# The tail of an attention and SwiGLU backward pass: how pairs of token tiles are scaled, summed and copied

## The chip, the cores and the metric

The kernel runs on one core of one Trainium2 chip. A core has a matrix engine (TensorE, PE in the profile, with PEld for its weight loads), VectorE (DVE), ScalarE (ACT), GpSimd (POOL), a queue engine that issues transfers (SyncE, SP), and 16 DMA engines. The engines run side by side, each its own instructions in order, and wait for each other by semaphores. The on-chip memories are SBUF (128 partitions) and PSUM, into which TensorE writes its results. The metric is the time of one execution on the device in microseconds (us); runs are summed up by their median.

## The reference

A transformer block with both branches on the same normalised input, and the gradients of its inputs. S = 2048 tokens, D = 448, 16 heads of 28, F = 1792, everything bfloat16.

```python
xn = layernorm(x)                      # no weights, eps 1e-5
qkv = xn @ wqkv                        # 448 x 1344
p = softmax(q @ k.T * 28 ** -0.5);  o = p @ v
out = x + o @ wo + (silu(xn @ w_gate) * (xn @ w_up)) @ w_down
grads = vjp(out)(grad_out)             # for x, wqkv, wo, w_gate, w_up, w_down
```

The outputs are out and six gradients. What matters here: with dqkv the gradient of q, k and v, the gradient of wqkv is xn^T dqkv, and the gradient of xn is dqkv wqkv^T plus the part from the FFN. With g that sum for one token, the gradient of x is rstd * (g - mean(g) - xn * mean(g * xn)) + grad_out.

## The kernel before

The forward pass (0 to about 618 us) computes attention for four groups of four heads and, as filler work between, the FFN. Then comes the turn, and the backward pass of attention: 512 steps, each a group g, a pair of heads hp, a chunk kc of 512 keys, a chunk qc of 512 queries and a tile qi of 128 queries. `row(k)` computes scores and dP of a step on TensorE, `ew(k)` the exponential on ScalarE and ds = dP * e on VectorE (L842), `kv(k)` accumulates dk and dv, and `dq_unit(b)` dq for a block of four steps. dq needs ds transposed. For the tiles 0 to 2 of a block a DMA does this (`dst_dma`, issued by SP, L823 and L827), for tile 3 TensorE, in `tr_unit` (L878, copied by ScalarE at L879). Between the steps TensorE gets filler units (y, FFN part of dx, and `dc_unit`, L1149), in an order that is written out by hand.

At the turn, the pieces of the last units of the forward pass (`last[-5:]`: 16 pieces of dO wo^T, L482; three of small VectorE work; 16 of the gradient of wo, L518) are taken one by one, counted in n, and the steps 0 to 3 of the backward pass are started between them, when n % 8 == 1.

After the last step comes the tail (from about 1429 us), for 16 tiles of 128 tokens in eight pairs:

- `dx_a(t0)` sums the gradient of xn in PSUM (tile "tok", six buffers). dqT (L1273) and dkv (L1277) are the last group's. The rest of the sum already lies in SBUF as dxg (fp32). For an even tile VectorE adds dxg and sums the row (L1291); for an odd one TensorE adds dxg by a matmul with the identity in fp32 (L1280), and ScalarE sums the row (gs, L1288). In both cases VectorE forms the product with xn and its row sum (pr, L1294); its input is dxg in SBUF for an even tile and tok in PSUM for an odd one.
- `dx_b(t)`, one pair later, scales the two row sums by rstd and -1/D (two [128, 1] instructions of VectorE, L1301), forms t1 on ScalarE (L1304) and t2 on VectorE (L1307), adds them on GpSimd (L1309) and stores the tile (SP, L1310). t1 and t2 take turns in five buffers called e_sb.
- The list `rest` holds the last group's weight gradient of wqkv: two `dsp_unit` and two `dsq_unit` (8 transposes each and a copy by VectorE, L978 and L959) and four `dwq_unit` (16 matmuls of 384 columns, L988, and four casts by VectorE, L994 to L997). Two units are taken in each iteration over t, one behind each place of a `dx_b`, from the first iteration on (which has no `dx_b` yet), so all eight are through after four iterations: the four of transposes at t = 0 and 2, two `dwq_unit`s at t = 4 and two at t = 6.

Of the kernel before, what the change touches and what calls it, by code (L numbers as in the profile page):

```python
# [9 lines left out]
ALU = mybir.AluOpType  # L10
# [20 lines left out]
CH = 256  # L31
NCH = S // CH
QH = 256
LO = 44
HOT = 150

# [66 lines left out]
def kernel(  # L103
# [222 lines left out]
    def run(u):  # L326
        for _ in u:
            pass
# [501 lines left out]
    def ew(k):  # L830
        if k < NB:
            est[k] = kq.tile([P, 2, 512], BF16, name="e_sb", bufs=5)
            for j in range(2):
                ACTE.activation(out=est[k][:, j], in_=sps.pop((k, j))[:], func=ACT.Exp, scale=SCALE)  # L834
        if 1 <= k <= NB:
            g, hp, kc, qc, qi = steps[k - 1]
            b = (k - 1) // 4
            if qi % 2 == 0:
                dss[k - 1] = dss[k] = kq.tile([P, 2, 2, 512], BF16, name="ds_sb", bufs=5)
            ds = dss[k - 1]  # L840
            for j in range(2):
                DVE.tensor_tensor(out=ds[:, qi % 2, j], in0=dps.pop((k - 1, j))[:], in1=est[k - 1][:, j], op=ALU.mult)  # L842
            if qi == 1 or qi == 2:
                if bk is None:
                    pend.append(lambda: dst_dma(b, ds, qi))
                else:
                    dst_dma(b, ds, qi)
# [10 lines left out]
    for u in last[-5:]:  # L858
        for _ in u():
            n += 1  # L860
            if n % 8 == 1 and k < 4:
                row(k)
                ew(k)
                k += 1
# [8 lines left out]

    def tr_unit(b):
        ds = dss.pop(4 * b + 3)
        ps = ps_b.tile([P, 8, P], BF16, name="db", bufs=3)
        for c in range(8):
            PE.transpose(ps[:, c, :], ds[:, 1, c // 4, (c % 4) * P:(c % 4 + 1) * P], ident_bf[:])  # L878
        ACTE.copy(out=dsT[b][:, 3].rearrange("p j kt s -> p (j kt) s"), in_=ps[:])  # L879

    def kv(k):
        g, hp, kc, qc, qi = steps[k]
# [83 lines left out]
    def dsp_unit(g, kind, t8, tag="genb"):  # L966
        if g not in dsp:
            need(lambda: g == 0 or (g - 1, 3) in s_done)
        if g not in dsp:
            dsp[g] = bk.tile([P, NT, 3, P], BF16, name="dsp", bufs=1)  # L970
        src = dkv[g, kind - 1]
        ps = (ps_b if tag == "rest" else ps_g).tile([P, 8, P], BF16, name=tag, bufs=2 if tag == "rest" else 1)
        for j in range(8):
            t = 8 * t8 + j
            PE.transpose(ps[:, j, :], src[:, t * P:(t + 1) * P], ident_bf[:])
            if j < 7:
                yield 60
        DVE.tensor_copy(out=dsp[g][:, 8 * t8:8 * t8 + 8, kind, :], in_=ps[:])  # L978
        s_done.add((g, kind, t8))
        yield 60  # L980

# [2 lines left out]
    def dwq_unit(g, c, tag="genb"):  # L984
# [6 lines left out]
                yield 162  # L991
        o = bk.tile([P, 3, 4, DH], BF16, name="dwq_o")
        p4 = ps[:].rearrange("p (k h r) -> p k h r", k=3, r=HP)
        DVE.tensor_copy(out=o[:dn, 0], in_=p4[:dn, 0, :, :DH])  # L994
        DVE.tensor_copy(out=o[:dn, 1:3, 0:2, :], in_=p4[:dn, 1, :, :DH].rearrange("p (k h) r -> p k h r", k=2))
        DVE.tensor_copy(out=o[:dn, 2, 2:4, :], in_=p4[:dn, 2, 0:2, :DH])
        DVE.tensor_copy(out=o[:dn, 1, 2:4, :], in_=p4[:dn, 2, 2:4, :DH])  # L997
        store(wq_out[d0:d0 + dn, :, g * 4 * DH:(g + 1) * 4 * DH],
              o[:dn].rearrange("p k h r -> p k (h r)"))
        s_done.add((g, c))  # L1000
# [262 lines left out]
    g = G - 1  # L1263
    both = [(dkv[g, 0], wqT[:, 3 * g + 1]), (dkv[g, 1], wqT[:, 3 * g + 2])]

    def dx_a(t0):
        for t in (t0, t0 + 1):
            pst = ps_b.tile([P, 512], FP32, name="tok", bufs=6)
            psd[t] = pst[:, :D]
        for hp in range(2):  # L1270
            for t in (t0, t0 + 1):
                r = 64 * (t % 2)
                PE.matmul(psd[t], lhsT=dqT[g][r:r + 64, hp, t // 2 * P:(t // 2 + 1) * P], rhs=dxs["wqd"][r:r + 64, hp],  # L1273
                          start=(hp == 0), stop=False, tile_position=(r, 0), skip_group_check=True)
        for t in (t0, t0 + 1):
            for i, (l, r) in enumerate(both):
                PE.matmul(psd[t], lhsT=l[:, t * P:(t + 1) * P], rhs=r, start=False, stop=(i == 1 and t % 2 == 0),  # L1277
                          skip_group_check=True)
            if t % 2:
                PE.matmul(psd[t], lhsT=ident_f[:], rhs=dxs["g"][:, t, :], start=False, stop=True, skip_group_check=True)  # L1280
        for t in (t0, t0 + 1):
            ps = psd[t]
            sa = tw.tile([P, 1], FP32, name="sa", bufs=6)
            sb = tw.tile([P, 1], FP32, name="sb", bufs=6)
            sms[t] = (sa, sb)
            if t % 2:
                gs = tw.tile([P, D], BF16, name="gs")
                ACTE.activation(out=gs[:], in_=ps, func=ACT.Identity, accum_out=sa[:])  # L1288
            else:
                psd[t] = dxs["g"][:, t, :]  # L1290
                DVE.scalar_tensor_tensor(out=psd[t], in0=ps, scalar=1.0, in1=psd[t],  # L1291
                                         op0=ALU.mult, op1=ALU.add, accum_out=sa[:])
            pr = tw.tile([P, D], BF16, name="pr")
            DVE.scalar_tensor_tensor(out=pr[:], in0=psd[t], scalar=1.0, in1=xn_sp[:, t, :],  # L1294
                                     op0=ALU.mult, op1=ALU.mult, accum_out=sb[:])

    def dx_b(t):
        ps = psd.pop(t)
        sa, sb = sms.pop(t)
        for x in (sa, sb):  # L1300
            DVE.tensor_scalar(out=x[:], in0=x[:], scalar1=rstd[:, t:t + 1], scalar2=-1.0 / D,  # L1301
                              op0=ALU.mult, op1=ALU.mult)
        t1 = kq.tile([P, 512], FP32, name="e_sb", bufs=5)[:, :D]
        ACTE.activation(out=t1, in_=ps, func=ACT.Identity, scale=rstd[:, t:t + 1], bias=sa[:])  # L1304
        t2 = kq.tile([P, 512], FP32, name="e_sb", bufs=5)[:, :D]
        dy = dy2[t // 4][:, t % 4, :] if t < 8 else dy4[:, t - 8, :]
        DVE.scalar_tensor_tensor(out=t2, in0=xn_sp[:, t, :], scalar=sb[:], in1=dy, op0=ALU.mult, op1=ALU.add)  # L1307
        dx = tw.tile([P, D], BF16, name="dx")
        POOL.tensor_tensor(out=dx[:], in0=t1, in1=t2, op=ALU.add)  # L1309
        SP.dma_start(out=out1_d[:, t, :], in_=dx[:])  # L1310

    rest = [dsp_unit(g, 2, t8, "rest") for t8 in range(2)]
    rest += [dsq_unit(g, hp, "rest") for hp in range(2)]
    rest += [dwq_unit(g, c, "rest") for c in range(4)]
    for t in range(0, NT + 2, 2):
        if t < NT:
            dx_a(t)
        for u in (t - 2, t - 1):
            if u >= 0:
                dx_b(u)  # L1320
            if rest:
                run(rest.pop(0))
    for u in rest:
        for _ in u:
            pass
    tlst.close()
    dxgst.close()
    bwd.close()
# [30 lines left out]
```

## Time and profile before

| what | us |
|---|---|
| median of 12 runs | 1484.97 |
| lowest and highest of them | 1481.98, 1496.54 |
| the profiled execution | 1483.37 |
| its span, first to last instruction | 1481.6 |
| busy: PE, ACT, DVE, POOL | 1350.0, 1262.8, 1159.3, 361.4 |
| tail, from the first L1273 to the end of the span | 1429.65 to 1481.6 |
| start of the last store (L1310) | about 1478.6 |

A profile is one execution. Its rows give the start and the duration of instructions in microseconds from the span's start. Durations of neighbouring rows of one engine overlap a little, so what an instruction occupies is better read from the starts. "x4" is a count; in brackets stands how long the engine was idle before, and who ended it. L12 is line 12 of the kernel before. In the page's shares, an engine's share of the whole span says little about the tail: there PE is at 0 from about 1461 on. PEclk is the clock that TensorE was granted, as a share of full speed.

### The profile page before, as it was taken

Reading aid. Unit: us, or ns where it says so; the run is one execution under the profiler, and the core shown is the slowest. Engines: PE = TensorE matmul, PEld = TensorE weight load, DVE = VectorE, ACT = ScalarE, POOL = GpSimd, SP = SyncE. Lnnn points to the kernel's source line nnn. Section 1 sums busy time; section 2 is a strip of 40 time slices with the busy share of each in tenths; the row PEclk is TensorE's granted clock in tenths of the full one; section 3 lists DMA queues with packets and bytes.
Section 4 is the critical chain, followed back from the end, with each engine's and each line's share of the span. In section 5 each row is a group of like instructions: output and inputs, shape, how many; then the busy total and the mean of one; then the engine's idle time right before and its main releaser. Section 6 shows DMA issues by size and latency. Waiting matters only on the chain. (4 is left out here: it accounts for less than half of the span.)

```text
span 1481.6 us, 34337 instructions
## 1 busy us (share of the span) xinstructions
PE 1350.0 (91%) x12672; PEld 542.2 (37%) x12672; DVE 1159.3 (78%) x2030; ACT 1262.8 (85%) x2180; POOL 361.4 (24%) x487
## 2 busy tenths in 40 slices
PE   5899999889999999888999889999999998999994
PEld 2333333333333333323333334433343343443341
DVE  6677666556666766587888879888889999999987
ACT  5798989888999998688888879899889998889953
POOL 6474423463434444101001001001001010000113
PEclk9999999999999999988999989999999999999997
DMA  5797856696788676699999999999999999999961
GB/s 149 171 209 184 206 117 157 158 209 161 154 179 189 138 173 142 169 204 195 203 198 201 206 206 189 196 208 215 215 186 200 203 211 214 199 194 211 185 122 50
DMA packets 698591, 269.55 MB, mean 182 GB/s; under 512 B 618080, under 2 KB 674104, under 8 KB 698424
## 3 DMA queue, kind: packets, MB, share of 16 engines
q1 hardware_dynamic: 693448, 261.24, 86.5%
q0 software_dynamic: 3568, 5.83, 1.7%
q8 instruction: 99, 1.62, 0.5%
q14 instruction: 68, 0.56, 0.1%
q10 hardware_dynamic: 1408, 0.30, 0.1%
HBM read 63.99 MB, written 58.85 MB: 83 GB/s over the span
## 5 line engine op out<-in xcount | busy, mean ns | idle before, releaser
L842 DVE TENSOR_TENSOR ds_sb<-db,e_sb 128x512 bf16<-128x512 f32 x1024 | 648.3, 684 | 70.9 <-PE db L815 29.2
L834 ACT ACTIVATE e_sb<-sb 128x512 bf16<-128x512 f32 x1024 | 554.1, 611 | 62.2 <-PE db L815 45.3
L608 ACT ACTIVATE eT<-s_w 128x1024 bf16<-128x1024 f32 x256 | 263.4, 1029 | 49.1 <-PE s_ps L605 46.3
L610 ACT ACTIVATE eT<-s_ps 128x512 bf16<-128x512 f32 x512 | 280.2, 612 | 0.0
L815 PE MATMUL db<-kd,qd 32*128 32x512 bf16 x1024 | 242.3, 389 | 17.1 <-DVE ds_sb L842 16.2
L807 PE MATMUL sb<-kd,qd 32*128 32x512 bf16 x1024 | 214.1, 392 | 5.5 <-ACT e_sb L834 3.3
L938 POOL TENSOR_TENSOR dq_acc<-dq_acc,dq_st 128x256 f32<-128x256 f32 x64 | 46.5, 727 | 586.2 <-ACT dq_st L936 586.2
L896 PE MATMUL acc<-ds_sb,qd 128*32 128x512 bf16 x1024 | 165.2, 400 | 0.0
L892 PE MATMUL acc<-e_sb,qd 128*32 128x512 bf16 x1024 | 163.2, 400 | 1.6 <-DVE dw_o L523 1.6
L879 ACT COPY dsT<-db 128x1024 bf16<-128x1024 bf16 x128 | 130.1, 1017 | 28.6 <-PE db L878 27.7
L377 POOL TENSOR_TENSOR nn<-nn,ag 128x512 f32<-128x512 f32 x56 | 71.3, 1272 | 247.2 <-DVE ag L375 237.6
L605 PE MATMUL s_ps<-QQ,KK 32*128 32x512 bf16 x512 | 125.9, 385 | 4.1
L1105 PE MATMUL genb<-wguT,dau_c 128*128 128x448 bf16 x448 | 117.5, 355 | 6.3 <-ACT dq_st L936 3.3
L605 PE MATMUL s_w<-QQ,KK 32*128 32x512 bf16 x512 | 100.3, 387 | 11.6 <-ACT eT L608 10.0
L807 PEld LDWEIGHTS <-qd 32*128 32x128 bf16 x1024 | 48.3, 91 | 149.7 <-issue 140.8
L416 PE MATMUL gen<-xn_t,f_sp 128*128 128x448 bf16 x448 | 98.5, 354 | 1.2 <-DVE hda L405 1.1
L923 PE MATMUL genb<-dsT,kd 128*32 128x256 bf16 x2048 | 82.8, 284 | 7.3 <-DVE y L1057 3.8
L416 PEld LDWEIGHTS <-f_sp 128*128 128x128 bf16 x672 | 58.7, 98 | 81.5 <-issue 29.6
L878 PE MATMUL db<-ident_bf,ds_sb 128*128 128x128 bf16 x1024 | 80.5, 223 | 1.8 <-DVE ds_sb L842 1.8
L878 PEld LDWEIGHTS <-ds_sb 128*128 128x128 bf16 x1024 | 69.1, 100 | 27.4 <-issue 8.8
L378 POOL TENSOR_TENSOR nn<-nn,tt 128x512 f32<-128x512 f32 x56 | 71.8, 1283 | 4.4
L923 PEld LDWEIGHTS <-kd 128*32 128x32 bf16 x2048 | 56.9, 100 | 43.7 <-issue 15.5
(157 smaller groups left out, 1882.3 us busy)
## 6 DMA issues: line engine op xcount, KB each, us to landing
F_d<-hda SPq DMA_DIRECT2D x56, 384.0 KB
dau_c<-F_d SPq DMA_DIRECT2D x56, 256.0 KB
h_c<-F_d SPq DMA_DIRECT2D x24, 256.0 KB
qd<-QD_d SPq DMA_DIRECT2D x24, 256.0 KB
dc<-dqkvT_d SPq DMA_DIRECT2D x12, 384.0 KB
dsT<-ds_sb SPq DMA_TRANSPOSE x256
wT_d<-wT_f SPq DMA_DIRECT2D x14, 256.0 KB
KD_d<-qk_sp SPq DMA_DIRECT2D x7, 512.0 KB
```

The costliest lines, as they stand in the source:

```text
L416: PE.matmul(ps[:, :D], lhsT=fsp[fc][:, t // 4, w, t % 4, :], rhs=rhs[:, t, :], start=(t == 0), stop=(t == NT - 1))
L605: PE.matmul(sp4[hh], lhsT=KK[g][r:r + HP, kt * P:(kt + 1) * P], rhs=QQ[g][r:r + HP, qsl], start=True, stop=True, tile_position=(r, 0))
L608: ACTE.activation(out=e2[0][:], in_=wide[:], func=ACT.Exp, scale=SCALE)
L610: ACTE.activation(out=e2[1][:, j], in_=sp4[2 + j], func=ACT.Exp, scale=SCALE)
L807: PE.matmul(s_ps[:], lhsT=qside[g, qc][r:r + HP, 0, qi * P:(qi + 1) * P], rhs=kside[g, kc][r:r + HP, 0, :], start=True, stop=True, tile_po ...
L815: PE.matmul(d_ps[:], lhsT=qside[g, qc][r:r + HP, 1, qi * P:(qi + 1) * P], rhs=kside[g, kc][r:r + HP, 1, :], start=True, stop=True, tile_po ...
L834: ACTE.activation(out=est[k][:, j], in_=sps.pop((k, j))[:], func=ACT.Exp, scale=SCALE)
L842: DVE.tensor_tensor(out=ds[:, qi % 2, j], in0=dps.pop((k - 1, j))[:], in1=est[k - 1][:, j], op=ALU.mult)
L878: PE.transpose(ps[:, c, :], ds[:, 1, c // 4, (c % 4) * P:(c % 4 + 1) * P], ident_bf[:])
L892: PE.matmul(a[r:r + HP, :], lhsT=sp4[:, 1, r:r + HP], rhs=e[:, j, :], start=first, stop=last, tile_position=(0, r), skip_group_check=True)
L896: PE.matmul(a[r:r + HP, :], lhsT=sp4[:, 0, r:r + HP], rhs=ds[:, qi % 2, j, :], start=first, stop=last, tile_position=(0, r), skip_group_ch ...
L923: PE.matmul(ps[r:r + HP, :256], lhsT=ks[:, kt, h:h + HP], rhs=t[:, par::2, j, kt, :], start=(kt == 0), stop=(kt == 3), tile_position=(0, r ...
```

## The change

Six edits:

1. At the turn, steps 0 to 3 are started at n = 8, 17, 25 and 32 instead of 1, 9, 17 and 25.
2. In the last block of the backward pass tile 2 of ds is transposed by TensorE too; its copy is made by VectorE. SP issues one transposition less.
3. Tiles 0, 2, 4 and 6 to 12 (EVEN) add dxg on VectorE; 1, 3, 5, 13, 14 and 15 by the matmul with the identity. So of the pairs (6, 7), (8, 9) and (10, 11) both tiles are summed on VectorE, and of (14, 15) none.
4. The four row sums of a pair lie in one [128, 2, 2] tile and are scaled by one instruction, against nrs = -rstd / D, made once by GpSimd. t2 gets buffers of its own (ds_sb), dx four. The last tile's addition is on VectorE. In `dx_a` the dqT matmuls come last.
5. The units of `rest` stand behind both `dx_b` of an iteration: two each at t = 0 and 2, then one `dwq_unit` each at t = 4, 6, 8 and 10 (before: two each at t = 0, 2, 4 and 6).
6. The four casts of the last `dwq_unit`s, and the second copy of `dsp_unit`, are made by ScalarE.

```diff
-            if qi == 1 or qi == 2:
+            if qi == 1 or qi == 2 and b < NB // 4 - 1:
...
-            if n % 8 == 1 and k < 4:
+            if n in (8, 17, 25, 32):
...
+        for qi in (3,) if b < NB // 4 - 1 else (2, 3):
+            ps = ps_b.tile([P, 8, P], BF16, name="db", bufs=3)
+            for c in range(8):
+                PE.transpose(ps[:, c, :], ds[:, qi % 2, c // 4, (c % 4) * P:(c % 4 + 1) * P], ident_bf[:])
+            o = dsT[b][:, qi].rearrange("p j kt s -> p (j kt) s")
+            if qi == 2:
+                DVE.tensor_copy(out=o, in_=ps[:])
+            else:
+                ACTE.copy(out=o, in_=ps[:])
...
+        (ACTE.copy if tag == "rest" and t8 else DVE.tensor_copy)(out=dsp[g][:, 8 * t8:8 * t8 + 8, kind, :], in_=ps[:])
...
+        cp = ACTE.copy if tag == "rest" else DVE.tensor_copy
+        cp(out=o[:dn, 0], in_=p4[:dn, 0, :, :DH])
...
+    nrs = tw.tile([P, NT], FP32, name="nrs", bufs=1)
+    POOL.tensor_scalar(out=nrs[:], in0=rstd[:], scalar1=-1.0 / D, scalar2=None, op0=ALU.mult)
...
     def dx_b(t):
         ps = psd.pop(t)
-        sa, sb = sms.pop(t)
-        for x in (sa, sb):
-            DVE.tensor_scalar(out=x[:], in0=x[:], scalar1=rstd[:, t:t + 1], scalar2=-1.0 / D,
-                              op0=ALU.mult, op1=ALU.mult)
+        sm = sms[t - t % 2]
+        if t % 2 == 0:
+            DVE.tensor_tensor(out=sm[:], in0=sm[:], in1=nrs[:, t:t + 2].unsqueeze(2).to_broadcast([P, 2, 2]), op=ALU.mult)
+        sa, sb = sm[:, t % 2, 0:1], sm[:, t % 2, 1:2]
...
-        t2 = kq.tile([P, 512], FP32, name="e_sb", bufs=5)[:, :D]
+        t2 = kq.tile([P, 2, 512], FP32, name="ds_sb", bufs=5)[:, 0, :D]
...
-        dx = tw.tile([P, D], BF16, name="dx")
-        POOL.tensor_tensor(out=dx[:], in0=t1, in1=t2, op=ALU.add)
+        dx = tw.tile([P, D], BF16, name="dx", bufs=4)
+        (DVE if t == NT - 1 else POOL).tensor_tensor(out=dx[:], in0=t1, in1=t2, op=ALU.add)
...
+    at = {0: 2, 2: 2, 4: 1, 6: 1, 8: 1, 10: 1}
     for t in range(0, NT + 2, 2):
         if t < NT:
             dx_a(t)
         for u in (t - 2, t - 1):
             if u >= 0:
                 dx_b(u)
-            if rest:
-                run(rest.pop(0))
+        for _ in range(at.get(t, 0)):
+            run(rest.pop(0))
```

## The prediction, made before the changed kernel was run

> **What bounds the kernel now.** I read the table of busy time by stretches first, to find where the engines stop being full; then the chain that ended last; then the tail's order of time, row by row.
>
> ```profile
> 1410.00:1420.00 10.00, 10.00 (x114) 4.14 (x117) 9.83 (x18) 9.47 (x18) 1.00 (x2) 1.00 0.91 130
> 1420.00:1430.00 10.00, 8.08 (x110) 3.70 (x102) 5.55 (x12) 5.22 (x8) 0.00 (x0) 0.83 0.88 160
> 1444.00:1448.00 4.00, 4.00 (x24) 1.93 (x23) 2.29 (x10) 0.64 (x2) 1.13 (x1) 1.00 0.37 100
> 1464.00:1468.00 4.00, 0.00 (x0) 0.00 (x0) 3.73 (x12) 1.53 (x3) 1.79 (x2) 0.58 0.17 57
> 1472.00:1476.00 4.00, 0.00 (x0) 0.00 (x0) 3.68 (x10) 1.71 (x4) 2.55 (x3) 0.50 0.09 30
> ```
>
> The columns are the stretch, its length, and the busy time of PE, PEld, DVE, ACT and POOL, then PE's clock, the DMA share and GB/s. Up to 1420 three engines are full, and the change leaves the instructions of that loop as they are. At 1444 to 1448 PE is full and DVE half idle; from 1464 PE has nothing left and DVE alone is full. So the tail has a stage set by PE (about 1444 to 1458) and one set by DVE (1458 to 1477). The chain that ended last is DVE work to the end but for the last POOL addition:
>
> ```profile
> 1475.93 1.40 DVE e_sb L1307
> 1477.33 0.03 POOLq L1309
> 1477.36 0.07 issue
> 1477.43 1.15 POOLq L1354
> ```
>
> One pair of token tiles in the stage of DVE, from the tail in order of time (start, duration, engine, line, instruction):
>
> ```profile
> 1463.59 0.61 DVE L1291 SCALAR_TENSOR_TENSOR dxg<-tok,dxg 128x448 f32<-128x448 f32 x1
> 1463.80 1.13 POOL L1309 TENSOR_TENSOR dx<-e_sb 128x448 bf16<-128x448 f32 x1 [0.61 <-ACT gs L1288]
> ...
> 1464.24 1.17 DVE L1294 SCALAR_TENSOR_TENSOR pr<-dxg,xn_t 128x448 bf16<-128x448 f32 x1
> ...
> 1465.34 0.61 DVE L1294 SCALAR_TENSOR_TENSOR pr<-tok,xn_t 128x448 bf16<-128x448 f32 x1
> ...
> 1466.32 0.68 DVE L1307 SCALAR_TENSOR_TENSOR e_sb<-xn_t,sb,dsT 128x448 f32<-128x448 bf16 x1
> ...
> 1467.14 1.13 POOL L1309 TENSOR_TENSOR dx<-e_sb 128x448 bf16<-128x448 f32 x1 [2.21 <-DVE sa L1301]
> ...
> 1467.37 1.38 DVE L1307 SCALAR_TENSOR_TENSOR e_sb<-xn_t,sb,dsT 128x448 f32<-128x448 bf16 x1
> ```
>
> The same L1307 takes 0.68, or 1.38 when an addition of POOL is running; L1294 takes 0.61 with its input from PSUM and 1.17 when both inputs are in SBUF and POOL is running. 1467.37 to 1468.75 ends 0.48 after POOL's 1467.14 + 1.13 = 1468.27, most of a free instruction: DVE waited for POOL. From dxg to dxg a pair takes 1468.67 - 1463.59 = 5.08.
>
> **The change, part by part.** Starts of neighbouring DVE rows give what each occupies: dxg 0.65 with its accumulator row, a product 0.55, a last scaling (L1307) 0.61, a small scaling (L1301) 0.12, plus 0.1 until the next instruction sees it.
>
> *Turn from forward to backward (the condition on n).* Rows 0 to 3 go behind the 8th, 17th, 25th and 32nd piece of work, not the 1st, 9th, 17th and 25th. The first matmul that needs the accumulators waits for the copy of dw_o, which DVE does at 627.42. From 620.44 on DVE has no gap before that copy, and the work before it is the same, only in another order; its one idle stretch (0.55, before 620.44) becomes about 0.4, the time until PE has done all 16 pieces and the product can start. Gain 0.15. The small operations of the last forward block move ahead of two ds products, so SP gets its transposition 1.2 earlier; it is hidden, nobody waits for SP before 640. I take 0.2, with -2 to +2, for what a shifted start may do to transfers.
>
> *Last ds by TensorE.* SP loses one transposition (1.94 of issue), PE gains 8 transposes (0.53 to 0.9 by the rows of L878), DVE one copy of 128x1024 (0.68, row L978). PE does wait for that transfer: L923 waits 1.24 and starts at 1429.10. But look at what is late next: PE starts the transposes at 1426.33, 16 of them last until 1427.75; the dq matmuls of the block before run to 1428.4 and DVE's dqT after them to 1428.92 (0.42), and only then is the one PSUM bank free; ScalarE's copy of the last quarter ends at 1429.06. So the last dq starts at 1429.1 as before: 0, between -0.5 (PE at full clock) and +0.5.
>
> *Tail, PE.* Two of the eight additions of dxg by an fp32 matmul go (0.76 each in starts), the dqT matmuls come last in a tile, and after the first pairs there is one dwq unit (2.7 by L988: 16 matmuls) in an iteration instead of two. Before, an iteration had 2 x 2.7 + 2.0 = 7.4 (the starts at 1444.82 and 1452.23 are 7.41 apart); now it has 2.7 + 1.25 = 3.95 and is below DVE's.
>
> *Tail, ScalarE.* 16 casts of dwq_o and one 128x1024 copy come from DVE, two gs go. A copy of 128x256 takes 0.38 to 0.43 (L936) and 448 columns 0.54 (L1288), so 112 columns about 0.26 and 56 about 0.22: some 0.75 to 1.0 a unit. ScalarE was busy 1.5 of 4. What is queued behind a unit's casts is the next pair's t1, or gs of tile 13; the matmuls they wait for end 3 us before their turn. Hidden; without that cover each unit would cost up to 1.
>
> *Tail, DVE.* 32 small scalings go for 8 of 128x4 (0.24 each with the wait for it); 16 casts and one copy go (4 x 0.62 + 0.62); 2 dxg of 0.65 come, and the last addition (0.6). A pair whose two tiles are both summed on DVE is then 2 x (0.65 + 0.555) + 0.24 + 2 x 0.61 = 3.87, without POOL.
>
> *POOL against DVE.* [...] The row: DVE's two-input instruction waits until POOL's addition ends, and the 16 additions last 1.13 each:
>
> ```profile
> L1309 POOL TENSOR_TENSOR dx<-e_sb x16: 1127/1130/1137, 1437.3 to 1477.5; 128x448 bf16<-128x448 f32 x16
> L378 POOL TENSOR_TENSOR nn<-nn,tt x56: 1264/1271/1592, 56.4 to 594.5; 128x512 f32<-128x512 f32 x56
> ```
>
> By the first of these alone POOL is never held. [...] The 1592 of L378 beside its median of 1271 is a hint that POOL can be held; I take both directions. Then such a pair runs: addition 1 starts at the end of the second t2; dxg 0.65; the product waits 1.13 - 0.65 = 0.48; when it ends, addition 2 starts; dxg, again 0.48. 3.87 + 2 x 0.48 = 4.83. With DVE held and POOL never held, additions start 0.5 earlier, and the tail below ends some 3.2 earlier.
>
> Now the stretches, each to the end of a t2 (before: rows of L1307; after: the instructions of each engine laid end to end in their new order with the durations above).
>
> - 1429.65 to t2 of tile 3 (1444.07): 14.4. After: PE reaches the end of its second pair 5.25 in (two pairs of 2.0, two transposing units of 0.53); then DVE does two products, scaling, two t2, two copies, dxg, the held product (0.44), a product, scaling, two t2: 8.1. Sum 13.4.
> - to tile 7 (1458.59): 14.5, set by PE. After: two DVE pairs, 9.7.
> - to tile 9 (1463.67): 5.1. After: 4.8.
> - to tile 11: 5.1. After, with tile 13 summed by TensorE: 0.65 + 0.48 + 0.555, then addition 2 holds the scaling for 1.13, + 0.24 + 1.22 = 4.3.
> - to tile 13 (1473.83): 5.1. After: the scaling waits for two additions, 2 x 1.13 + 0.08, + 0.24 + 1.22 = 3.8.
> - to the last addition (1478.58): 4.75. After: addition, t2, addition alternate: 1.26 + 1.13 + 2 x 0.61 + 1.13 + 0.62 = 5.4. The last addition on DVE saves 0.5 here.
>
> Sum 49.0 before, 41.4 after: 7.6 less. The store behind it keeps its 3.0 (1478.6 to 1481.6). With the turn, 7.8 off the span of 1481.6, giving 1473.8. That execution took 1483.37; the median of the runs is 1484.97, 1.6 above. Subtracting from the median: 1477.2.
>
> **Rivals.** *POOL is never held*, as its 16 equal rows suggest: 11.0 off, 1474. *The gain is cut by half*: the two sums on DVE bring two held products to each pair, four pairs in the middle; if DVE must also let POOL's second addition go first (another 1.13 for each of three pairs), 7.8 - 3.4 = 4.4 remains: 1480.5. [...] For it speaks that DVE idles behind POOL already; against it, that DVE's instruction asks first, 0.48 ahead. *Slower*: the clock of PE after the turn. Its rows:
>
> ```profile
> 640.00:650.00 10.00, 8.90 (x101) 3.35 (x101) 7.54 (x14) 8.90 (x17) 0.00 (x0) 0.83 1.07 195
> 650.00:660.00 10.00, 7.93 (x80) 3.00 (x78) 8.81 (x15) 9.18 (x18) 0.00 (x0) 0.96 1.06 198
> 660.00:664.00 4.00, 4.00 (x41) 1.19 (x42) 2.28 (x4) 2.75 (x6) 0.00 (x0) 0.50 1.22 210
> ```
>
> At half clock PE is full and DVE does 2.28 in 4 us instead of about 3.5, a loss of 0.35 us per us. [...] It decides from 8 / 0.35 = 23 more us at half clock, and with 35 the time is 1489. Against it: PE's idle gap at the turn (1.55) doesn't grow.
>
> **How the numbers follow.** As worked out, 0.60 (1475 to 1479.5); POOL not held, 0.12 (1472.5 to 1475); cut by half, 0.21 (1479.5 to 1483); slower, 0.07. The range leaves out the last and the ends of the second and third: 1473 to 1482.5. A measurement of this kernel tells about 0.3%, 4.5 us, from no change; faster therefore means below 1480.5. Faster: 0.60 + 0.12 + 0.08 = 0.80; same: 0.13; slower: 0.07.
>
> **What would show it.** Right: tail pairs of 4.8 between equal t2 rows in the middle; PE's last matmul near 1459 and no more full stretch of PE after 1445; POOL's first addition of a pair starting at the end of the second t2; the last dq matmuls still near 1429.1; the last DVE addition near 1471. Wrong: additions that start while a t2 runs and keep 1.13 (POOL not held, faster); products of 1.7 or scalings waiting over 1.2 (cut by half); DVE rows waiting for gs or PE for casts on ScalarE; a backward loop that reaches 1420 later than before (clock).

## The result, and the profile after

The changed kernel takes 1469.94 us (median of 11 runs, 1467.69 to 1474.87) against 1484.52 us (median of 47 runs of the kernel before, 1474.93 to 1496.54): a ratio of 0.9903, 95% interval 0.9886 to 0.992, that is 11.9 to 16.9 us less. The forecast was 7.8 us less, with a range of 1473.0 to 1482.5. The direction was right, the size was not.

The profiled execution took 1469.94 us, its span 1468.1 (before 1481.6). Where the 13.5 us between the two spans lie, in marks that both traces have:

| from, to | before | after | less |
|---|---|---|---|
| start of the span, last ds product (L842, L843 after) | 1423.85 | 1421.91 | 1.94 |
| last ds product, last dq matmuls (L923, L929 after) | 5.25 | 3.70 | 1.55 |
| last dq matmuls, first matmul of the tail | 0.55 | 0.55 | 0 |
| first matmul of the tail, end of the span | 51.95 | 41.94 | 10.01 |

"The tail" below is always the last of these rows. The first row scatters by several us from execution to execution, as is shown further down; the last hardly does.

The busy time by stretches of the changed kernel (columns as before: stretch, length, PE, PEld, DVE, ACT, POOL, clock, DMA share, GB/s), at places that answer to those shown before:

```profile
1410.00:1420.00 10.00, 10.00 (x121) 4.00 (x120) 9.83 (x18) 9.53 (x18) 0.99 (x2) 1.00 1.01 160
1420.00:1430.00 10.00, 8.72 (x118) 5.24 (x117) 6.16 (x14) 4.70 (x8) 0.00 (x0) 1.00 0.77 188
...
1446.00:1450.00 4.00, 4.00 (x27) 2.20 (x25) 3.82 (x10) 1.91 (x6) 2.40 (x3) 1.00 0.28 79
...
1454.00:1458.00 4.00, 1.41 (x7) 0.32 (x6) 3.22 (x8) 2.56 (x8) 2.95 (x4) 0.92 0.24 68
1458.00:1462.00 4.00, 0.00 (x0) 0.00 (x0) 3.78 (x9) 1.92 (x5) 2.95 (x4) 0.50 0.18 57
```

Where DVE was half idle beside a full PE (busy 2.29 of 4 us), it is now at 3.82 of 4. PE ends at 1455.4, 29.25 after the tail's first matmul (before 31.69), and DVE carries the rest. The chain that ended last is DVE's last addition:

```profile
1463.66 0.09 issue
1463.75 0.05 DVEq L1319
1463.80 0.04 issue
1463.84 1.28 DVE dx L1319
```

One pair whose two tiles are both summed on DVE, in order of time (start, duration, engine, line, instruction; "x2" is two instructions in one row):

```profile
1447.43 1.28 DVE L1317 SCALAR_TENSOR_TENSOR ds_sb<-xn_t,sm,dsT 128x448 f32<-128x448 bf16 x2
1448.35 2.83 POOL L1319 TENSOR_TENSOR dx<-e_sb,ds_sb 128x448 bf16<-128x448 f32 x2 [1.60 <-ACT e_sb L1314]
1448.63 0.62 DVE L1301 SCALAR_TENSOR_TENSOR dxg<-tok,dxg 128x448 f32<-128x448 f32 x1
...
1449.29 0.90 DVE L1304 SCALAR_TENSOR_TENSOR pr<-dxg,xn_t 128x448 bf16<-128x448 f32 x1
...
1450.12 0.61 DVE L1301 SCALAR_TENSOR_TENSOR dxg<-tok,dxg 128x448 f32<-128x448 f32 x1
...
1450.78 0.89 DVE L1304 SCALAR_TENSOR_TENSOR pr<-dxg,xn_t 128x448 bf16<-128x448 f32 x1
...
1451.85 1.28 DVE L1317 SCALAR_TENSOR_TENSOR ds_sb<-xn_t,sm,dsT 128x448 f32<-128x448 bf16 x2
```

From t2 to t2 a pair takes 1451.85 - 1447.43 = 4.42, where 4.83 was forecast and 5.08 stood before. The two t2 of this pair are not held: 1.28 together. POOL's first addition starts 0.92 behind the first t2, into the second one, and is itself held: the two additions take 2.83 instead of 2 x 1.13. The products wait for POOL, but take 0.90 and 0.89 instead of 0.62: a wait of 0.28, not the 0.48 of the forecast. The additions and these products over the whole kernel (shortest, median, longest in ns):

```profile
L1319 POOL TENSOR_TENSOR dx<-e_sb,ds_sb x15: 1123/1357/1515, 1434.2 to 1463.3; 128x448 bf16<-128x448 f32 x15
...
L1304 DVE SCALAR_TENSOR_TENSOR pr<-dxg,xn_t x10: 624/890/1118, 1429.0 to 1453.7; 128x448 bf16<-128x448 f32 x10
```

Before, the additions were 1127/1130/1137. So POOL is held now, for the first time in this tail.

### The profile page after: what moved, and what is told of

Same layout as the page of the kernel before. It is cut to its first block, busy times and chain, and to the rows that moved or that the text cites. A ratio compares the mean times of both kernels' runs of the same rounds, so it can differ in the third digit from the quotient of the medians.

```text
span 1468.1 us, 34327 instructions
## 1 busy us (share of the span) xinstructions
PE 1349.8 (92%) x12676; PEld 541.7 (37%) x12676; DVE 1152.6 (79%) x1995; ACT 1264.1 (86%) x2193; POOL 362.3 (25%) x487
## 5 line engine op out<-in xcount | busy, mean ns | idle before, releaser
L843 DVE TENSOR_TENSOR ds_sb<-db,e_sb 128x512 bf16<-128x512 f32 x1024 | 648.4, 684 | 70.0 <-PE db L816 33.1
L929 PE MATMUL genb<-dsT,kd 128*32 128x256 bf16 x2048 | 82.6, 283 | 5.4 <-DVE y L1064 2.9
L929 PEld LDWEIGHTS <-kd 128*32 128x32 bf16 x2048 | 56.9, 100 | 41.6 <-issue 15.3
```

Of the source, the lines that this page charges most:

```text
L929: PE.matmul(ps[r:r + HP, :256], lhsT=ks[:, kt, h:h + HP], rhs=t[:, par::2, j, kt, :], start=(kt == 0), stop=(kt == 3), tile_position=(0, r ...
```

## The experiments

The theory that the runs were to test: the gain lies in the tail and comes of the pair on DVE (one scaling, copies on ScalarE, the units of weight gradients apart), with POOL and DVE each made to wait for the other. ("Port" in what was expected of the runs is the author's word for whatever the two wait for; the runs show who waits and for how long, not at what.) The rivals: the gain comes of the turn or of the last ds; or the tail's gain has one cause alone. The tail of three executions with the same tail code and TensorE at full clock (the changed kernel, the run without the new turn, the run with needless transposes below) is 41.94, 41.99 and 41.94. One execution is therefore enough for a difference of half a us in the tail, though not for the time of the whole kernel.

**The parts alone.** Four kernels, each against the same 37 runs of the kernel before (median 1484.86).

The tail edits (3 to 6) alone: the changed kernel with the turn, the issue of the last ds and `tr_unit` as before:

```diff
-            if n in (8, 17, 25, 32):
+            if n % 8 == 1 and k < 4:
...
-            if qi == 1 or qi == 2 and b < NB // 4 - 1:
+            if qi == 1 or qi == 2:
```

> The tail's edits alone, without the turn's and without the last ds on TensorE. Theory A (the tail carries nearly all): the two traces give 49.0 us before and 39.5 after from the last dq to the last addition, so 9.5 to 10.5 off the median. Theory B (the tail gave what was forecast, 7.6, and the rest lies in the loop or the last ds): 7 to 8.

Measured: 1475.05 us (median of 6), ratio 0.9914 (0.9893 to 0.9936). The tail is 42.86, and the last dq starts 5.25 behind the last ds product.

The new turn alone, put into the kernel before:

```diff
-            if n % 8 == 1 and k < 4:
+            if n in (8, 17, 25, 32):
```

> The kernel before with only the turn's condition changed. Theory A: 0, within 1. Theory B (the new start of the backward loop is worth what the trace of after is ahead at its end, 2 to 3 us): 2 to 3.5 off.

Measured: 1482.89 us (16 runs), ratio 0.9986 (0.9969 to 1.0002), which includes no change.

The last ds by TensorE alone, put into the kernel before, with the changed `tr_unit`:

```diff
-            if qi == 1 or qi == 2:
+            if qi == 1 or qi == 2 and b < NB // 4 - 1:
```

> The kernel before with only the last block's third tile transposed by TensorE. My forecast of this step was 0, because PE would only start the last dq at the same time. By the trace of after it starts 1.5 earlier in relation to the last ds product. Theory A (the gain is real: without the transfer PE goes on at full clock and without the 1.24 wait): 1 to 2 off, and the last dq starts 5.2 behind the last ds product. Theory B (TensorE's clock fell at that place in the trace of before by chance): 0 to 0.5, and the start depends on the clock.

Measured: 1484.08 us (22 runs), ratio 0.9978 (0.9958 to 0.9998): at the edge of what can be told; the two medians differ by only 0.8 us. Its last dq came 5.05 behind the last ds product, with a stretch of half clock between the two.

All but the turn:

```diff
-            if n in (8, 17, 25, 32):
+            if n % 8 == 1 and k < 4:
```

> The changed kernel with the turn as before. Theory A: the time of the changed kernel, 1469 to 1471. Theory B: 2 to 3.5 more, 1472 to 1473.5.

Measured: 1470.16 us (4 runs), ratio 0.9887 (0.9871 to 0.9902), tail 41.99. It can't be told from the changed kernel. The tail carries the gain; the turn adds nothing that can be told, the last ds little.

**Each edit of the tail put back.** Four kernels, one execution each: the changed kernel with one edit undone.

The weight-gradient units two at a time again:

```diff
-    at = {0: 2, 2: 2, 4: 1, 6: 1, 8: 1, 10: 1}
+    at = {0: 2, 2: 2, 4: 2, 6: 2}
```

> The changed kernel with the units of the weight gradient as before: two each in the iterations t = 0, 2, 4, 6. Length of the tail = from the first matmul of the first pair to the end of the span: 51.95 before (1429.65 to 1481.6), 41.94 after (1426.16 to 1468.1). Theory A (one unit per pair takes PE out of the bound): 3.5 to 4.5 longer, PE full between 1440 and 1450. Theory B (DVE's savings carry the gain, the place of the units matters little): under 1 longer.

Measured: tail 46.45, 4.5 more. The groups by shape say why: sums of DVE wait 8.4 us for TensorE instead of 2.9. First the changed kernel,

```profile
L1301 DVE SCALAR_TENSOR_TENSOR dxg<-tok,dxg 128x448 f32<-128x448 f32 x10 | 6.2, 618 | 2.9 <-PE tok L1291 2.9
```

then the run (the numbers behind the bars: busy us and mean ns of one; idle us before them and who ended it):

```profile
L1301 DVE SCALAR_TENSOR_TENSOR dxg<-tok,dxg 128x448 f32<-128x448 f32 x10 | 6.2, 620 | 8.4 <-PE tok L1291 8.4
```

Casts and copy of the last units on VectorE again:

```diff
-        (ACTE.copy if tag == "rest" and t8 else DVE.tensor_copy)(out=dsp[g][:, 8 * t8:8 * t8 + 8, kind, :], in_=ps[:])
+        DVE.tensor_copy(out=dsp[g][:, 8 * t8:8 * t8 + 8, kind, :], in_=ps[:])
...
-        cp = ACTE.copy if tag == "rest" else DVE.tensor_copy
+        cp = DVE.tensor_copy
```

> The changed kernel with the last weight gradients' casts and the second copy of dsp back on VectorE. Theory A (DVE is the bound of every pair, so its work counts in full): 4 casts units of 0.62 and a copy of 0.62 make 2.5 to 3.1 longer. Theory B (DVE waits for POOL's port anyway and the casts, which read PSUM, fill these waits): under 1.5 longer.

Measured: tail 44.35, 2.4 more, just under what DVE's own instructions come to.

Which tiles DVE sums, as before:

```diff
-EVEN = (0, 2, 4, 6, 7, 8, 9, 10, 11, 12)
+EVEN = (0, 2, 4, 6, 8, 10, 12, 14)
```

> The changed kernel with dxg added by VectorE for every even tile and by TensorE for every odd one. PE gets four fp32 additions of 0.76 back in the pairs that share it with a weight gradient unit (3.95 to 4.7 there), loses two; DVE loses 0.1 per exchanged tile and the wait of the product for POOL (0.28), but waits for ScalarE's row sum. Theory A: 0.5 to 1.5 longer, PE the bound of the pairs from 1440 to 1456. Theory B (the second held product costs more than PE): 0.5 to 1 shorter.

Measured: tail 43.56, 1.6 more.

Two small scalings for each tile, between the two t2, as before:

```diff
-        if t % 2 == 0:
-            DVE.tensor_tensor(out=sm[:], in0=sm[:], in1=nrs[:, t:t + 2].unsqueeze(2).to_broadcast([P, 2, 2]), op=ALU.mult)
         sa, sb = sm[:, t % 2, 0:1], sm[:, t % 2, 1:2]
+        for x in (sa, sb):
+            DVE.tensor_scalar(out=x, in0=x, scalar1=rstd[:, t:t + 1], scalar2=-1.0 / D,
+                              op0=ALU.mult, op1=ALU.mult)
```

> The changed kernel with two scalings of [128, 1] per tile again, in the same place, in place of one for the pair. Theory A (in full): four small instructions of 0.12 and two waits of 0.1 against one of 0.27, 0.45 per pair, 8 pairs: 3 to 3.6 longer. Theory B (swallowed by the waits for POOL): under 1.5 longer.

Measured: tail 50.68, 8.7 more, which no theory had. Undoing the smallest edit takes back most of the gain. The four rows that say how, from the order of time of this run:

```profile
1447.95 0.69 DVE L1318 SCALAR_TENSOR_TENSOR ds_sb<-xn_t,sm,dsT 128x448 f32<-128x448 bf16 x1
1448.55 0.33 DVE L1312 TENSOR_SCALAR sm<-sm,rstd 128x1 f32<-128x1 f32 x2
1448.87 1.13 POOL L1320 TENSOR_TENSOR dx<-e_sb,ds_sb 128x448 bf16<-128x448 f32 x1 [3.74 <-DVE sm L1312]
1448.99 1.49 DVE L1318 SCALAR_TENSOR_TENSOR ds_sb<-xn_t,sm,dsT 128x448 f32<-128x448 bf16 x1
```

The scalings push the second t2 to 1.04 behind the first. POOL's addition comes at 0.92, 0.12 us ahead of it, and the t2 takes 1.49 instead of 0.69. Then POOL's second addition meets the next product (1.27), and a pair takes 5.96 (t2 at 1447.95 and at 1453.91) instead of 4.42. All 15 additions are back at 1.13. The four undone edits add up to 17.2 us, more than the 10.0 that all bring, so they are not independent.

New theory A: what the single scaling is worth is mostly the order in which the second t2 and POOL's first addition start. Rival B: this run was slow for its own instructions and waits. The next runs put needless instructions of VectorE between the t2's; their result, in a tile of its own, is not used.

```diff
+        for i in range(2 * (t % 2)):
+            DVE.tensor_scalar(out=pad[:, 4 * t + i:4 * t + i + 1], in0=rstd[:, t:t + 1], scalar1=1.0, scalar2=None,
+                              op0=ALU.mult)
         DVE.scalar_tensor_tensor(out=t2, in0=xn_sp[:, t, :], scalar=sb, in1=dy, op0=ALU.mult, op1=ALU.add)
```

> The changed kernel with two needless instructions of [128, 1] (0.12 each, their results unused) between the two t2 of a pair. POOL's first addition starts 0.92 after the first t2 starts (1447.43 and 1448.35 in the changed kernel); the second t2 comes at 0.61 + 0.25 = 0.86, still ahead of it. Theory A (who asks first holds the port): only the instructions' own time, 8 x 0.25, so the tail goes from 41.94 to 43.5 to 44.2. Theory B (no such threshold, small instructions cost much by themselves): 4 or more longer.

Measured: tail 42.92, 1.0 more. With three in place of two:

> Three such instructions: the second t2 comes at 0.61 + 0.37 = 0.98, behind POOL's addition (0.92). Theory A: the second t2 is held by the addition for some 0.8 in most pairs (1.49 in place of 0.69), and the tail jumps by 4 to 6 over the run with two, to 48 to 50, near the 50.7 of the run with two scalings per tile. Theory B: another 1.0 over the run with two.

Measured: tail 43.47, 1.5 more. This was no test of A: I had priced an instruction at 0.12, and they occupy about 0.06 each, so the second t2 came near 0.8, still ahead of POOL. The mean addition of POOL went from 1332 ns to 1397 and 1429: POOL was held longer. Four needless instructions:

> The changed kernel with four needless [128, 1] operations of VectorE ahead of the second t2 of each pair. By the runs with two and three they occupy about 0.065 us each, so the second t2 comes some 0.87 us after the first, still ahead of POOL's first addition (0.91 to 0.92 after the first t2). Both theories: the tail (first tail matmul to the end of the span) is 43.9 to 44.5 us, against 41.9 for the changed kernel, POOL's additions stay longer than 1.13 in the mean and the second t2 stays near 0.69 where it is ahead. If the margin of 0.05 us is too small, some pairs tip over.

Measured: tail 44.03, mean addition 1425 ns. One of the eight pairs tipped over. There POOL's addition started 0.01 us ahead of the second t2, and the t2 was held:

```profile
1441.87 0.69 DVE L1321 SCALAR_TENSOR_TENSOR ds_sb<-xn_t,sm,dy 128x448 f32<-128x448 bf16 x1
...
1442.71 1.14 POOL L1323 TENSOR_TENSOR dx<-e_sb,ds_sb 128x448 bf16<-128x448 f32 x1 [1.98 <-ACT e_sb L1315]
1442.72 1.61 DVE L1321 SCALAR_TENSOR_TENSOR ds_sb<-xn_t,sm,dy 128x448 f32<-128x448 bf16 x1
```

Seven:

> As before with seven needless operations: the second t2 comes 1.05 us after the first, behind the start of POOL's first addition. Theory A (who reaches the shared port first decides): POOL's additions are all 1.13 again, the median t2 is about 1.48, and the tail jumps to 47.5 to 51 us. Theory B (the run with two small scalings between the t2's was slow for its own instructions and waits, the order at the port is of no weight): 0.5 us for each needless operation, as in the runs with two and three, so 45.0 to 45.8 us.

Measured: tail 49.28, 7.3 more, where four gave 2.1. The rows (in order of time, then by line in ns):

```profile
1451.15 0.69 DVE L1321 SCALAR_TENSOR_TENSOR ds_sb<-xn_t,sm,dsT 128x448 f32<-128x448 bf16 x1
1451.76 0.51 DVE L1317 TENSOR_SCALAR pad<-rstd 128x1 f32<-128x1 f32 x7
1452.07 1.13 POOL L1323 TENSOR_TENSOR dx<-e_sb,ds_sb 128x448 bf16<-128x448 f32 x1 [2.81 <-ACT e_sb L1315]
1452.19 1.50 DVE L1321 SCALAR_TENSOR_TENSOR ds_sb<-xn_t,sm,dsT 128x448 f32<-128x448 bf16 x1
```
```profile
L1323 POOL TENSOR_TENSOR dx<-e_sb,ds_sb x15: 1127/1131/1615, 1434.2 to 1470.4; 128x448 bf16<-128x448 f32 x15
```

The median t2 there is 904 and not the 1480 that was expected: the first t2 of a pair stays free, and half of them are first ones.

Not all of the 7.3 need come of t2 being held. TensorE waited longer for its first weight-gradient unit here, and a stretch of half clock followed (1437.99 to 1441.40), so that the unit took 4.38 instead of 2.76. First the changed kernel, then this run:

```profile
1435.85 2.76 PE L994 MATMUL rest<-dsp,xn_t 128*128 128x384 bf16 x16 [1.53 <-DVE dsp L965]
```
```profile
1437.04 4.38 PE L994 MATMUL rest<-dsp,xn_t 128*128 128x384 bf16 x16 [2.76 <-DVE dsp L965]
```

DVE waits for TensorE once after it, 1.46 instead of 0.78, so the clock explains at most 1.5 of the 7.3. The next three pairs, in which DVE doesn't wait for TensorE, are each 1.2 to 1.4 longer than in the changed kernel. The run with the old scalings has the same stretch (idle 2.87, the unit 4.44, then a wait of 1.29).

The same seven ahead of the first t2 of the pair (the factor t % 2 becomes 1 - t % 2), so that the t2 stay back to back:

> The same seven needless operations for each pair, but ahead of the first t2 of the pair, so that the two t2 stay back to back. Theory A: the operations cost their own time only, 45.0 to 45.8 us, POOL's additions stay longer than 1.13 and the median t2 is 0.68. Theory B: the same as with the seven between the t2's.

Measured: tail 43.76, 1.8 more, even less than expected. The median addition is as in the changed kernel:

```profile
L1323 POOL TENSOR_TENSOR dx<-e_sb,ds_sb x15: 1121/1357/1520, 1431.8 to 1462.4; 128x448 bf16<-128x448 f32 x15
```

Same instructions, same number, 5.5 us apart by their place, and still 4.0 if the clock is given all of its 1.5. A holds, B falls.

**Is it POOL at all?** All 16 additions on VectorE:

```diff
-        (DVE if t == NT - 1 else POOL).tensor_tensor(out=dx[:], in0=t1, in1=t2, op=ALU.add)
+        DVE.tensor_tensor(out=dx[:], in0=t1, in1=t2, op=ALU.add)
```

> The changed kernel with all 16 additions on VectorE; GpSimd has no work in the tail. Theory A (POOL holds DVE's two-input instructions): every product from dxg takes 0.62 and every t2 0.69; a pair is 3.87 + 2 x 0.6 = 5.1 plus what an addition waits for t1, against 4.42, and the tail is 3 to 5 longer. Theory B (the longer rows have another cause): products of 0.9 remain.

Measured: tail 47.14, 5.2 more, a little above the forecast. Half clock comes in this tail too (1437.69 to 1441.10, behind an idle stretch of 3.05; the unit takes 4.44), but DVE's wait for TensorE behind it, 0.79, is that of the changed kernel. With POOL gone every row has its short length, so that POOL is what lengthens them (by line, in ns: t2, product):

```profile
L1317 DVE SCALAR_TENSOR_TENSOR ds_sb<-xn_t,sm,dsT x12: 679/682/686, 1446.0 to 1469.2; 128x448 f32<-128x448 bf16 x12
...
L1304 DVE SCALAR_TENSOR_TENSOR pr<-dxg,xn_t x10: 624/625/626, 1429.3 to 1459.8; 128x448 bf16<-128x448 f32 x10
```

**The clock at the tail's start.** The run of the tail edits alone had 0.9 more in the tail than the changed kernel, and the run of the turn alone 1.0 more than the kernel before. In both TensorE is idle for 2.5 us or more while it waits for the transfer of the last ds, and the first matmuls behind it run at half clock (the row of the last dq is 1.04 and 1.05, against 0.62). By the stretches of the run of the tail edits alone:

```profile
1432.00:1434.00 2.00, 1.24 (x17) 0.65 (x18) 0.08 (x1) 0.00 (x0) 0.00 (x0) 0.58 1.10 339
1434.00:1436.00 2.00, 2.00 (x6) 0.98 (x4) 0.35 (x1) 0.00 (x0) 0.00 (x0) 0.57 1.09 334
```

To see whether the idle stretch is the cause, the last ds went by DMA again, and 24 needless transposes, their result unused, kept TensorE busy:

```diff
+        if b == NB // 4 - 1:
+            ps = ps_b.tile([P, 8, P], BF16, name="db", bufs=3)
+            for c in range(24):
+                PE.transpose(ps[:, c % 8, :], ds[:, 1, c % 8 // 4, (c % 4) * P:(c % 4 + 1) * P], ident_bf[:])
```

> The changed kernel without its edit of the last ds (tile 2 of the last block goes by DMA again), and with 24 needless transposes of TensorE ahead of the last two dq units, their result unused, so that TensorE is not idle while the DMA lands. Theory A (the half clock at the start of the tail comes of that idle stretch): the last dq starts 5.2 to 5.5 us behind the last ds product as in every run with the DMA, but its row is 0.62 and not 1.04, and the tail is 41.9 to 42.3. Theory B (the half clock has another cause): row 1.04 and a tail of 42.8 or more.

Measured: the last dq 5.28 behind the last ds product, idle before it 1.30, its row 0.62, the tail 41.94. By stretches, at the same place:

```profile
1424.00:1426.00 2.00, 0.70 (x28) 0.39 (x20) 0.42 (x1) 0.00 (x0) 0.00 (x0) 1.00 0.87 220
1426.00:1428.00 2.00, 2.00 (x21) 0.80 (x10) 0.42 (x1) 0.00 (x0) 0.00 (x0) 1.00 1.06 347
```

This is what was expected if the idle stretch is the cause. It is one execution, beside two with the long idle stretch and the half clock, and the kernel before with an idle stretch of 1.24 and full clock behind it. The other traces fit in the tail: of TensorE's idle stretches of over 1 us there and just ahead of it, over all runs, the five of 2.50 to 3.05 us had half clock in them or within 1 us of their end, and none of the 19 from 1.1 to 2.31 did. In the loop they fit less well: in the kernel before, an idle stretch of 2.49 (845.67 to 848.16) had full clock behind it until 857.10, and half clock also comes there without such a stretch (in the changed kernel at 866.87 and 1136.53, with no idle stretch over 0.82 in the 10 us ahead). So the idle stretch is the likely cause in the tail, and not shown to be the only one.

**A version that might beat both.** The additions of the last four tiles on VectorE, and other tiles summed there:

```diff
-EVEN = (0, 2, 4, 6, 7, 8, 9, 10, 11, 12)
+EVEN = (0, 1, 2, 4, 5, 6, 7, 8, 9, 10, 12)
...
-        (DVE if t == NT - 1 else POOL).tensor_tensor(out=dx[:], in0=t1, in1=t2, op=ALU.add)
+        (DVE if t >= NT - 4 else POOL).tensor_tensor(out=dx[:], in0=t1, in1=t2, op=ALU.add)
```

> An attempt at a faster one: the changed kernel with the last four additions on VectorE, tile 1 and tile 5 summed on VectorE (so that the first pair doesn't wait for an fp32 addition on TensorE, 0.76) and tile 11 by TensorE. Laying the durations of the changed kernel end to end gives a tail 1.5 to 2.5 shorter, 39.5 to 40.5; the median 1467.5 to 1468.5. If the additions on DVE wait for ScalarE's t1 the tail is equal or longer.

Measured: tail 41.31, only 0.6 less than the changed kernel; ratio to the kernel before 0.9921 (0.9893 to 0.9949), so not shown to be faster than the changed kernel. The four additions on VectorE gain nothing: from the first t2 of tiles 12 and 13 to the end of the last addition it takes 5.94, against 5.90 in the changed kernel. The sum of tile 12 now waits 0.93 for TensorE.

## Why the prediction was off

**What failed.** Three terms of the sum were too small. DVE's waits for POOL in the tail were mis-sized: a held product waits 0.28 and not 0.48, and the tail's stretches sum to 38.9 and not to 41.4. The last ds by TensorE was put at 0 and is worth 1.0 to 1.55. The turn was put at 0.2 and is worth 0.4 to 0.7. Together that is some 4 of the 7 us by which the median lies under the forecast of 1477.2; the rest stays open.

**The sign and the place were right.** The tail's gain was forecast at 7.6 of 7.8 us, and the tail has 10.0 of the 13.5 between the spans. The order of the sizes of the stretches held too (each to the end of a t2; forecast, measured):

| stretch | forecast | measured |
|---|---|---|
| tail's start to tile 3 | 13.4 | 12.9 |
| to tile 7 | 9.7 | 9.6 |
| to tile 9 | 4.8 | 4.4 |
| to tile 11 | 4.3 | 3.9 |
| to tile 13 | 3.8 | 3.5 |
| to the last addition | 5.4 | 4.6 |
| sum | 41.4 | 38.9 |

Before the sum was 49.0; the store behind it kept its 3.0. Two of the rows need care. The agreement to tile 7 is luck: the second of its two pairs takes 4.4 instead of 4.83, but the first takes 5.2, because DVE waits 0.78 for TensorE's sum, a wait that the forecast didn't have:

```profile
1439.88 0.62 DVE L1301 SCALAR_TENSOR_TENSOR dxg<-tok,dxg 128x448 f32<-128x448 f32 x1 [0.78 <-PE tok L1291]
```

And the instructions listed for the first stretch come to about 7.5 by the prediction's own durations, not 8.1; the 8.1 fits with the sum of the second pair's even tile added, which does wait for TensorE (1431.36). The part took 7.8.

**Step "POOL against DVE": right that each waits for the other, the held product mis-sized.** The product waits 0.28 and not 0.48 in the pairs of the middle. The forecast let each engine hold the other until the recorded end of its row. But the second product of the pair shown begins, by its free duration, at 1450.78 + 0.89 - 0.62 = 1451.05, 0.13 ahead of the end of POOL's second addition (1448.35 + 2.83 = 1451.18). The first addition, whose row ends at 1449.70, begins at 1448.57, 0.14 ahead of the end of the second t2 (1447.43 + 1.28 = 1448.71) and 0.06 ahead of dxg, with which the forecast let it begin. The row shown before the result said the same: the t2 at 1467.37 took 1.38 where 0.68 is free, so it began at 1468.07, 0.20 ahead of POOL's recorded end at 1468.27. The prediction named the 0.48 that it ended behind POOL, called it "most of a free instruction" and didn't subtract. Two products in a pair make 2 x 0.20 = 0.4, and that is the whole difference between 4.83 and 4.42. The same 0.3 to 0.4 is missing in the stretches to tiles 11 and 13. In the last stretch the rows of both engines are lengthened:

```profile
1460.14 2.44 POOL L1319 TENSOR_TENSOR dx<-e_sb,ds_sb 128x448 bf16<-128x448 f32 x2 [1.05 <-ACT e_sb L1314]
1460.42 1.09 DVE L1311 TENSOR_TENSOR sm<-sm,nrs 128x4 f32<-128x4 f32 x1
1461.62 2.04 DVE L1317 SCALAR_TENSOR_TENSOR ds_sb<-xn_t,sm,dsT 128x448 f32<-128x448 bf16 x2
```

The row of the first t2 starts at 1461.62, inside POOL's second addition, and lasts 1.45. By its free duration of 0.68 it begins at 1462.38, 0.20 ahead of that addition's end (1462.58). Four such hand-overs in this stretch come 0.14 to 0.20 early, which is some 0.6 of the 0.8 between 5.4 and 4.6. No run shows the hold to the end of the other's row that the sum took, nor its waits of 1.13 and of 2 x 1.13 + 0.08 for the scalings ahead of tiles 11 and 13; those were the author's estimate. The two scalings took 0.53 and 0.34 (1455.09 and 1458.78), where one that is not held took 0.15 to 0.16.

**That POOL is held was counted as a loss alone.** The forecast put it 3.2 us behind the case in which POOL is never held. The runs show the waiting in both directions: the t2 goes from 0.69 to 1.49 behind POOL (median addition 1.13), and POOL's additions go to 1.36 in the median behind a t2. But where both t2 are back to back, it is POOL, busy for 19.7 of the tail's 41.9 us, that waits. The order that holds DVE instead costs 5.5 us, up to 1.5 of them perhaps by the clock (seven needless instructions between the t2's against the same seven ahead of them). The forecast's hold to the end of the other's row fits only roughly: the release comes 0.2 ahead of the end of POOL's row (in the run with seven needless instructions too: 1452.19 + 1.50 - 0.69 = 1453.00, against 1452.07 + 1.13 = 1453.20).

**Rival "POOL is never held": its number was nearer, its reason was wrong.** It gave 1474 by DVE alone being held. POOL's longest addition is 1.515 and the median 1.357, so POOL is held. The 16 equal rows of before said only that no addition had come second. *"Cut by half"* needed the products to let POOL's second addition go first; they take 0.9, not 1.7. A state in which DVE waits like that exists, though: in the run with the old scalings the t2 take 1.49 and the products 1.27. *"Slower"* needed more half clock in the loop: the time at half clock from the turn to the last matmul of the tail is 51 us in both profiled executions, where the rival decides from 23 more.

**Step "last ds by TensorE": a gain of 0 was forecast, of 0.5 at full clock; it was 1.55.** The order of time of PE, first before, then after:

```profile
1425.33 1.07 PE L923 MATMUL genb<-dsT,kd 128*32 128x256 bf16 x16
...
1426.33 0.98 PE L878 MATMUL db<-ident_bf,ds_sb 128*128 128x128 bf16 x8
...
1429.10 0.62 PE L923 MATMUL genb<-dsT,kd 128*32 128x256 bf16 x16 [1.24 <-DMA dsT<-ds_sb]
```
```profile
1422.75 0.71 PE L929 MATMUL genb<-dsT,kd 128*32 128x256 bf16 x16
1423.39 1.07 PE L880 MATMUL db<-ident_bf,ds_sb 128*128 128x128 bf16 x16
...
1425.61 0.62 PE L929 MATMUL genb<-dsT,kd 128*32 128x256 bf16 x16 [0.60 <-DVE dqT L938]
```

The profiled execution of before had a stretch of half clock just there (transposes 0.98 for 8, against 1.07 for 16 now). I took its rows, and the start at 1426.33, as the general case. At full clock the transposes start 1.48 behind the last ds product (1421.91) instead of 2.48, and the dq of the block before and its dqT follow sooner; the last dq then waits for dqT, as forecast, but at 3.70 and not at 5.25. Over all executions: by DMA 5.25 to 5.52 (four); by TensorE 3.70 in six at full clock, 4.2 in two, also at full clock, 5.0 to 5.1 in six with half clock there, on average 4.4. So the step is worth about 1 us in the mean; the forecast's 0 is what half clock makes of it. Not foreseen at all: in two of the four executions without this edit TensorE idles for 2.5 us or more and the tail starts at half clock (0.9 to 1.0).

**Step "turn": 0.15 was forecast for DVE's gap.** From the transposition of the accumulators to the copy of dw_o, before and after:

```profile
618.22 0.66 PE L462 MATMUL gen<-ident_f,oacc 128*128 128x128 f32 x4 [0.85 <-DVE oacc L454]
...
627.42 0.62 DVE L523 CAST dw_o<-gen 128x448 bf16<-128x448 f32 x1
```
```profile
619.32 0.66 PE L463 MATMUL gen<-ident_f,oacc 128*128 128x128 f32 x4 [0.85 <-DVE oacc L455]
...
628.12 0.61 DVE L524 CAST dw_o<-gen 128x448 bf16<-128x448 f32 x1
```

9.20 before and 8.80 after, 0.4 less. DVE's idle stretch gave 0.21 of it (0.55 before, 0.34 after); the work behind it also takes 0.19 less. Over all executions 9.20 to 10.19 with the old turn (four) and 8.79 to 9.46 with the new one (14), 0.7 less in the mean. The loop behind it, from this copy to the last ds product, takes 792.3 to 796.4 with the old turn and 789.6 to 798.2 with the new one: no effect on the loop can be told.

**What the sum leaves open.** Tail 10.0, last ds 1.0 to 1.55, turn 0.4 to 0.7: 11.4 to 12.3 us, against 11.9 to 16.9 measured. Up to some 3 us of the difference of the medians (14.6) have no place in these rows. Forward part and loop scatter by several us between executions of the same code, and these runs don't settle whether the rest is scatter or a small effect there.

**Of the signs named ahead:** PE's last matmul near 1459: 1455.4, which is right with the 3.5 by which the tail starts earlier. "No more full stretch of PE after 1445": wrong, PE shows 4.00 of 4 until 1454, beside a DVE at 3.8. POOL's first addition was to start at the end of the second t2: its row starts while it runs and is lengthened instead. The last dq near 1429.1 and the last DVE addition near 1471: 1425.61, and a last addition that ends at 1465.12.

## What to carry to other kernels

Where rows of VectorE and GpSimd lengthen when they meet, as here (t2 0.69 to 1.49, additions 1.13 to 1.36 in the median), look which of the two comes first at each meeting, and by how much. Here the margin was 0.3 us: four tiny instructions in it cost 2.1 us, and three further ones another 5.2 (up to 1.5 of them perhaps the clock's). The engine that has time to spare should be the one that waits. By its end less its free duration a held instruction began here 0.13 to 0.2 us ahead of the end of the other engine's row: subtract that before laying rows end to end, and before taking a row as the general case look at the granted clock at that very place.

## What the runs showed of the hardware

- The waits of the two engines for each other show as longer rows, on either engine: t2 0.69 to 1.49, GpSimd's addition 1.13 to as much as 1.61. By its free duration the instruction that waited began 0.13 to 0.2 us ahead of the end of GpSimd's row, and 0.14 ahead of the end of a t2.
- Needless [128, 1] instructions of VectorE, one behind the other without a wait, occupied about 0.06 us each (0.43 for seven), about half of the 0.12 that a small scaling between dependent instructions took.
- Half clock came in stretches of 3.41 us or multiples of it (up to 13.65), in the loop at other places in each of the two profiled executions; 10 of the 23 from the turn to the tail's last matmul had less than 1 us of idle TensorE in the 3.41 us ahead. In and just ahead of the tail, the five idle stretches of 2.50 to 3.05 us were met by half clock, and the shorter ones (1.1 to 2.31) were not. From 640 us on the longest idle stretch in the changed kernel is 3.28 (847.61 to 850.90), and half clock came in it, from 849.81.
